# Renewing sixteen operands eight slots apart instead of six, in a kernel of attention and Fourier mixing

## The chip, the core and the metric

The kernel runs on one core of a Trainium2 chip. The metric is the device time of one execution in microseconds (us): three runs before the change took 1754.96, 1755.81 and 1759.93, median 1755.81. One further execution was profiled: it took 1751.4, of which 1749.6 lie between its first and last instruction (the span) and 1.8 around them. All engine times below are of this one execution.

Engines are named as in the profile: PE multiplies matrices, DVE, ACT and POOL work on elements (VectorE, ScalarE, GpSimd), SP issues transfers. Each takes its own instructions in the order in which the program holds them.

## What is computed

Two mixings of the same `x` (2048 rows of 512, float32), joined by a gate per row:

```python
q, k, v = split(x @ wqkv)                          # 32 heads of 16
o = softmax(q @ k.T * scale) @ v                   # over all 2048 keys
a = o @ wo
re, im = x @ dft_hid_re.T, x @ dft_hid_im.T        # spectral part
b = dft_seq_re @ re - dft_seq_im @ im
g = sigmoid((x * gate_w).sum(-1))
out = g * a + (1 - g) * b
```

## The kernel before

**Stages.** The first 292 us or so project q, k and v and the hidden transforms `re` and `im`, which are stored in memory as `ab_d[0]` and `ab_d[1]` (sixteen row blocks of 128 rows each). Then the spectral products run until about 693 us of the span, and the attention over all heads follows until the end. Both earlier stages also carry scans: the maximum of every row of scores is needed before the softmax, and the products and maxima for it are placed beside the other work.

**Operands in two parts.** Every float32 operand is split in a rounded part and the rest of it (`ah`, `al`, or `hi`, `lo`), and a product is the sum of three: hi*hi, hi*lo, lo*hi. ACT copies the rounded part, DVE or POOL subtracts it from the raw operand.

**The spectral loop** (L551) goes over units of coefficients. A unit is 512 columns of one row block `t` of the cosine matrix (phase 0) or the sine matrix (phase 1), and is multiplied with four operands `s` (L585 to L589), three products each; so a unit is twelve products. POOL splits the coefficients three units ahead (L552, L313, L314), SP fetches them eight ahead (L553, L305). After the last unit of a row block ACT scales the two halves of the sum (tx and ty, L598, L602), and POOL adds them and, in phase 1, the stored sum of phase 0 (L546, L548).

**The change of parts.** The sixteen operands of phase 0 (`re`) lie in blocks which those of phase 1 (`im`) take over. So that blocks come free early, the last two row blocks of phase 0 and the first two of phase 1 are done by halves: (14, 0), (14, 1), (15, 0), (15, 1), then (14, 2), (14, 3), (15, 2), (15, 3), then in phase 1 (0, 0), (0, 1), (1, 0), (1, 1), and (0, 2), (0, 3), (1, 2), (1, 3), each pair being row block and quarter of the operands. In row block 15 (`swap`, L575) operand `s` has had its last use of phase 0, and its renewal is put on a list.

**Slots.** `beside()` is called once after each product (L589) and counts a slot. It first runs what is due (`run_due`, L208, by due slot and then by order of entry), then places the scan work. `after(n, f)` (L203) makes `f` due n slots later. What is due is only *placed* in its engine's order at that point; it then runs when that engine reaches it. Below, slot 0 is the start of unit (15, 0), whose first product is slot 1; phase 1 begins after slot 72.

**A renewal** (`renew`, L577) places three things: the copy `ah[s]` on ACT (L580), four slots later the subtraction `al[s]` on DVE (on POOL for s = 3, 7, 11, 15; L581, shown at L215 by the profile), and for s = 8 to 12 the load of operand s + 3 on SP (L286). Operands 0 to 7 are loaded ahead into two tiles (`early`, L570 to L574), 8 to 10 at slot 24 (L592, L593). Loads of 8 to 15 share three buffers (`abr`), so the load of s + 3 waits for the subtraction of s, and what stands behind that load in SP's order waits too.

**The scans beside.** About every third slot a scan is placed (`scan_folded`, L136): two score products on PE (L149), ACT's rectified copy of one into `fold` (L153), and DVE's addition and running maximum with the next (L155). Four score banks, `d0`, `d1`, `k0`, `k1`, have one buffer each: a product for a `d` bank waits for ACT's copy of two scans before, one for a `k` bank for DVE's maximum of two scans before. When a head pair's scans are complete, four small instructions finish its maxima on DVE (`shift`, L158: L170 to L173), four slots apart; one such group falls into this stretch, at slots 21, 25, 29 and 33.

Of the kernel before, what the change touches and what calls it, by code (L numbers as in the profile page):

```python
# [46 lines left out]
def build(tc, x, xT, wqkv, wo, wrT, wiT, cr, ci, gate, out):  # L47
    nc = tc.nc
    with ExitStack() as ctx:
# [34 lines left out]
        def row_loads(p, queue, keys=k_d):  # L84

            qs = stk.tile([P, S], F32R, tag="stk", name="qs")
            ks = stk.tile([P, S], F32R, tag="stk", name="ks")
            loads = []
            for j in range(2):
                b, r = 64 * j, slice(DH * ((2 * p + j) % 8), DH * ((2 * p + j) % 8) + DH)  # L90
                loads += [(ks[b:b + 32, :], keys[p // 4][r, 0:1, :].to_broadcast([DH, 2, S])),
                          (qs[b:b + 32, :], q_d[p // 4][r, :, :].rearrange("e n s -> (e n) s")),
                          (ks[b + 32:b + 48, :], keys[p // 4][r, 1, :]),
                          (qs[b + 32:b + 48, :], q_d[p // 4][r, 0, :])]
            return (qs, ks), [lambda dst=dst, src=src: queue.dma_start(dst.bitcast(F32), src) for dst, src in loads]
# [7 lines left out]
        def load_use(p):  # L103
            if p < NP:
                used[p], loads = row_loads(p, nc.sync)
                for load in loads:
                    load()
                qs, ks = used[p]
                for j in range(2):
                    b = 64 * j + 48  # L110
                    nc.sync.dma_start(ks[b:b + 2, :].bitcast(F32), ones_d)
                    for n in range(2):
                        nc.sync.dma_start(qs[b + n:b + n + 1, :].bitcast(F32),
                                          m_d[p][n:n + 1, :, j].rearrange("n g b k -> n b g k"))
# [61 lines left out]
        def halves_of(ps, lhs, rhs, first, last):  # L176

            for j in range(2):
                r = slice(64 * j, 64 * j + 64)
                nc.tensor.matmul(ps[j], lhs[r], rhs[r], start=first, stop=last)  # L180

        def block(i):
            return big.tile([P, 512], F32R, tag=f"b{i}", name=f"b{i}")
# [6 lines left out]
        with ExitStack() as pf:  # L190
# [8 lines left out]
            def xy():  # L199
                ps = psf.tile([P, 2, 512], F32, tag="xy", name="xy")  # L200
                return ps[:, 0, :], ps[:, 1, :]

            def after(n, f, *args):  # L203

                count[0] += 1
                due.append((slots[0] + n, count[0], f, args))
# [15 lines left out]
            def scan_at(spacing):  # L222
                pace[0] = spacing

            def beside():

                slots[0] += 1
                run_due()
                if pace[0] is None:
                    return  # L230
                pace[1] += (PACE / FOLD_PACE if seen[0] in FOLDED else 1.0) / pace[0]
                if seen[0] == FOLDED[0] and not beds:
                    pace[1] = 0.0
                while seen[0] < FRONT and pace[1] >= 1.0:
                    pace[1] -= 1.0
                    n = seen[0]
                    if n % SCANS == 36 and n - n % SCANS + SCANS < FRONT:
                        load_scan_beside(n // SCANS + 1)
                    if n not in FOLDED:
                        done = scan_plain(n)  # L240
                    else:

                        scan_folded(n, 0, *beds)
                        done = behind(n - 1)
                    seen[0] += 1
                    if seen[0] == FRONT:
                        done = behind(n)
                    if done is not None and done % SCANS == SCANS - 1:
                        for d, part in enumerate(shift(done // SCANS)):
                            after(3 + 4 * d, part)  # L250
# [33 lines left out]
            def load_operand(ph, s, pool):  # L284
                raw = pool.tile([P, D], F32, tag="raw", name="abr", bufs=3)
                nc.sync.dma_start(raw, ab_d[ph][s])  # L286
                return raw
# [19 lines left out]
            def prepare(n, copy=nc.gpsimd.tensor_copy, sub=nc.gpsimd.tensor_sub):  # L307
                if n >= len(coef):
                    return
                hi, lo = (cw.tile([P, 512], F32R, tag=tag, name=tag + "_").rearrange("p (c q) -> p c q", q=P)  # L310
                          for tag in ("chi", "clo"))
                raw = craw.pop(n)
                copy(hi, raw)  # L313
                sub(lo, raw, hi.bitcast(F32))  # L314
                ready[n] = hi, lo
# [212 lines left out]
            with ExitStack() as py:  # L528
                cp = py.enter_context(tc.tile_pool(name="cp", bufs=2, reuse_waits="tile"))
                def fetch(n):  # L530
                    if n < len(coef):
                        load_coef(n, cp.tile([P, CS, P], F32, tag="craw", name="craw", bufs=5))
# [18 lines left out]
                for n, (ph, t, u) in enumerate(coef):  # L551
                    prepare(n + 3)  # L552
                    fetch(n + 8)  # L553
                    if u == 0 and (ph, t) == (0, NB - 1):
                        scan_at(NARROW)
                    if u == 2 and (ph, t) == (1, 0):
                        scan_at(PACE)
                    if n == len(coef) - 2 * NU:
                        unfolded[FRONT // SCANS], loads = row_loads(FRONT // SCANS, nc.sync)
                        for load in loads:  # L560
                            load()
                        load_use(0)
                    hi, lo = ready.pop(n)
                    if u == 0:
                        pss[t] = xy()
                        if ph:
                            yre[t] = cp.tile([P, D], F32, tag="yre", name="yre")
                            nc.sync.dma_start(yre[t], y_d[t // 4][:, t % 4, :])
                    if (ph, t, u) == (0, NB - 3, 0):
                        for i in range(2):  # L570
                            raw = stk.tile([P, 4, D], F32, tag="stk", name="early")
                            for d in range(4):
                                early[4 * i + d] = raw[:, d, :]
                                nc.sync.dma_start(raw[:, d, :], ab_d[1][4 * i + d])  # L574
                    swap = (ph, t) == (0, NB - 1)  # L575

                    def renew(s):  # L577
                        raw = early.pop(s)
                        ah[s], al[s] = block(2 * s), block(2 * s + 1)
                        nc.scalar.copy(ah[s], raw)  # L580
                        after(4, (nc.gpsimd if s % 4 == 3 else nc.vector).tensor_sub, al[s], raw, ah[s].bitcast(F32))  # L581
                        if s >= 8 and s + 3 < NB:
                            early[s + 3] = load_operand(1, s + 3, cp)

                    for w in range(CS):  # L585
                        s = u * CS + w
                        for i, (c_, a_) in enumerate(((hi, ah[s]), (hi, al[s]), (lo, ah[s]))):
                            halves_of(pss[t], c_[:, w, :], a_, s == 0 and i == 0, s == NB - 1 and i == 2)
                            beside()  # L589
                        if swap:  # L590
                            if s == 7:
                                for i in range(8, 11):  # L592
                                    early[i] = load_operand(1, i, cp)  # L593
                            after(1 + 3 * (s % 8), renew, s)
                    if u == NU - 1:
                        tx = cp.tile([P, D], F32, tag="tx", name="tx")
                        ty = cp.tile([P, D], F32, tag="ty", name="ty")
                        nc.scalar.mul(tx, pss[t][0], gm[:, t:t + 1])  # L598
                        if n == len(coef) - 1:
                            nc.vector.tensor_scalar_mul(ty, pss[t][1], gm[:, t:t + 1])  # L600
                        else:
                            after(5, nc.scalar.mul, ty, pss[t][1], gm[:, t:t + 1])  # L602
                        after(10, mixed, ph, t, yre.get(t), tx, ty)
# [405 lines left out]
```

## Time and profile before

| | us |
|---|---|
| median of three runs | 1755.81 |
| profiled execution, its time | 1751.4 |
| its span | 1749.6 |
| PE busy in the span | 1719.9 |
| ACT busy | 1451.9 |
| DVE busy | 1155.1 |
| POOL busy | 712.7 |

The profile's timeline lists, per engine, start, duration, line and operation, what is written from what, how many alike were merged, and in square brackets the idle time ahead with what ended it. The table by windows gives, for a stretch of the span, each engine's busy time and instructions, and the TensorE clock that was granted (1.00 is full speed). Two score products or two half products run side by side on PE, so a row with x2 is one pair.

### The profile page before, as it was taken

What the parts mean: (1) busy time and instruction counts of PE and PEld (TensorE: products, weight loads), DVE (VectorE), ACT (ScalarE), POOL (GpSimd) and SP (SyncE); (2) the same over time, 40 slices, a digit from 0 to 9 for tenths busy, and PEclk for the clock granted to TensorE, in tenths of its full rate; (3) what the DMA queues carried; (4) which work ended last, traced back from release to release, by engine and by line L of the source; (5) the groups of instructions that cost most, each with busy time, mean ns of one, the idle gap of its engine ahead of it and who ended that gap; (6) DMA issues with size and microseconds to landing.
All of it is one profiled execution on the core that took longest, in us unless ns stands there. A gap on an engine that the chain in (4) does not pass through costs nothing.

```text
span 1749.6 us, 35589 instructions
## 1 busy us (share of the span) xinstructions
PE 1719.9 (98%) x13640; PEld 1021.8 (58%) x13640; DVE 1155.1 (66%) x1876; ACT 1451.9 (83%) x2384; POOL 712.7 (41%) x814
## 2 busy tenths in 40 slices
PE   8999999999999999999999999999999999999998
PEld 6887787888888887333333333333334555555554
DVE  6799999999999887666666666666664212222333
ACT  5445346888887887999999999999999888888885
POOL 3678667555556664032322323232232322322222
PEclk9999999999999999999999999999999999999999
DMA  8782666434354445433232423515313254255612
GB/s 296 254 298 79 190 201 206 121 115 117 104 154 140 139 133 120 74 59 63 58 67 56 82 40 64 95 23 99 78 35 73 64 118 90 68 141 137 177 36 100
DMA packets 126810, 199.55 MB, mean 114 GB/s; under 512 B 54016, under 2 KB 56560, under 8 KB 119728
## 3 DMA queue, kind: packets, MB, share of 16 engines
q1 hardware_dynamic: 84368, 161.02, 34.4%
q0 software_dynamic: 38496, 19.47, 5.2%
q10 hardware_dynamic: 3776, 16.78, 3.6%
q8 instruction: 107, 1.75, 0.4%
q14 instruction: 63, 0.52, 0.1%
HBM read 133.04 MB, written 63.71 MB: 112 GB/s over the span
## 4 chain that ended last, share of the span: by engine, by line
PE 89%; DMA 3%; DVE 3%; POOL 2%; issue 2%; ACT 1%; SPq 0%; DVEq 0%; ACTq 0%; POOLq 0%
PE pvb L660 28%; PE xy L180 21%; PE s L645 19%; PE s L180 8%; PE s L149 7%; PE s L130 6%; DVE mx L132 1%; DMA fa<-ks_d 1%; DMA kf_d<-fa 1%; POOL s L215 1%; DMA raws<-wqkv 0%; DMA raws<-xT 0%; POOL el L215 0%; POOL fa L215 0%; DMA abr<-ab_d 0%
## 5 line engine op out<-in xcount | busy, mean ns | idle before, releaser
L132 DVE TENSOR_REDUCE mx<-s 128x2 f32<-128x1024 f32 x524 | 627.2, 1222 | 207.5 <-PE s L130 207.4
L649 ACT ACTIVATE eb<-s 128x1024 f32<-128x1024 f32 x512 | 579.3, 1131 | 55.1 <-PE s L645 55.1
L653 ACT ACTIVATE e<-s 128x512 f32<-128x512 f32 x1024 | 610.3, 708 | 0.4 <-PE s L645 0.4
L660 PE MATMUL pvb<-e,va 128*17 128x512 f32 x2048 | 517.3, 598 | 0.0
L660 PE MATMUL pvb<-eb,va 128*17 128x512 f32 x2048 | 517.1, 598 | 0.0
L645 PE MATMUL s<-qs,ks 50*128 50x512 f32 x2048 | 428.1, 438 | 2.3 <-DVE ty L600 1.6
L645 PEld LDWEIGHTS s<-qs,ks 50*128 50x128 f32 x2048 | 212.6, 185 | 372.4 <-ACT eb L649 282.6
L155 DVE CUSTOM_DVE_ANT_0 fold<-s,fold 128x512 f32<-128x512 f32 x500 | 339.1, 690 | 39.0 <-PE s L149 19.4
L153 ACT ACTIVATE fold<-s 128x512 f32<-128x512 f32 x500 | 296.1, 602 | 70.0 <-PE s L149 43.1
L149 PE MATMUL s<-ks,qs 48*128 48x512 f32 x1000 | 223.3, 404 | 7.6 <-DVE mx L155 6.1
L130 PE MATMUL s<-ks,qs 48*128 48x512 f32 x1048 | 221.6, 396 | 3.7 <-DVE mx L132 2.5
L668 POOL DMA_DIRECT2D lc<-ob x124 | 63.1, 515 | 308.2 <-DVE ob L665 307.9
L660 PEld LDWEIGHTS pvb<-eb,va 128*17 128x17 f32 x2048 | 69.2, 96 | 190.2 <-issue 182.0
L149 PEld LDWEIGHTS s<-ks,qs 48*128 48x128 f32 x1000 | 120.9, 184 | 47.6 <-DVE mx L155 18.2
L675 POOL DMA_DIRECT2D r_d<-lc x31 | 18.1, 585 | 294.9 <-DVE lc L674 286.0
L130 PEld LDWEIGHTS s<-ks,qs 48*128 48x128 f32 x1048 | 108.3, 184 | 14.9 <-DVE mx L132 6.0
L180 PE MATMUL xy<-w,b 64*128 64x512 f32 x768 | 105.2, 392 | 0.2 <-ACT s L379 0.2
L401 ACT ACTIVATE tx<-xy 128x512 f32<-128x512 f32 x48 | 28.7, 599 | 78.6 <-PE xy L180 52.5
L754 DVE SCALAR_TENSOR_TENSOR y<-s,g,y 128x512 f32<-128x512 f32 x50 | 36.6, 748 | 76.6 <-PE s L180 76.0
L677 POOL DMA_DIRECT2D rb<-r_d x124 | 60.6, 496 | 63.0 <-DMA r_d<-lc 63.0
L180 PE MATMUL s<-b,chi 64*128 64x512 f32 x542 | 85.2, 390 | 0.3 <-ACT chi L963 0.3
L180 PEld LDWEIGHTS xy<-w,b 64*128 64x128 f32 x768 | 72.5, 186 | 17.6 <-ACT s L379 1.0
(750 smaller groups left out, 2320.4 us busy)
## 6 DMA issues: line engine op xcount, KB each, us to landing
craw<-ci SPq DMA_DIRECT2D x64, 256.0 KB
craw<-cr SPq DMA_DIRECT2D x60, 256.0 KB
ks<-k_d SPq DMA_DIRECT2D x46, 256.0 KB
qs<-q_d SPq DMA_DIRECT2D x46, 256.0 KB
ab_d<-ab SPq DMA_DIRECT2D x32, 256.0 KB
y_d<-y SPq DMA_DIRECT2D x32, 256.0 KB
o_d<-oh POOLq DMA_DIRECT2D x28, 256.0 KB, 9.8
o_d<-ol POOLq DMA_DIRECT2D x28, 256.0 KB, 11.9
```

The costliest lines, as they stand in the source:

```text
L130: nc.tensor.matmul(ps[:, j, :], qs[b:b + 48, qb * P:(qb + 1) * P], ks[b:b + 48, c * 512:(c + 1) * 512], start=True, stop=True)
L132: nc.vector.tensor_reduce(mx[p][:, :, qb, c], ps, axis=AX.X, op=ALU.max)
L149: nc.tensor.matmul(ps, qs[b:b + 48, qb * P:(qb + 1) * P], ks[b:b + 48, c * 512:(c + 1) * 512], start=True, stop=True)
L153: nc.scalar.activation(fold[j], ps, AF.Relu)
L155: nc.vector.tensor_tensor_reduce(out=fold[j], in0=ps, in1=fold[j], scale=1.0, scalar=-3.0e38, op0=ALU.add, op1=ALU.max, accum_out=mx[p][:, ...
L180: nc.tensor.matmul(ps[j], lhs[r], rhs[r], start=first, stop=last)
L645: nc.tensor.matmul(pss[j], ks[b:b + 50, kb * P:(kb + 1) * P], qs[b:b + 50, q0:q0 + 512], start=True, stop=True)
L649: nc.scalar.activation(e, ps, AF.Exp, scale=SCALE)
L653: nc.scalar.activation(e[j], pss[j], AF.Exp, scale=SCALE)
L660: nc.tensor.matmul(pvb[r:r + VC, :], va[:, kb, 2 * p + j, :], es[c][j], start=kb == 0, stop=kb == NB - 1, tile_position=(0, r))
L668: nc.gpsimd.dma_start(lc[32 * n:32 * n + 32, :], ob[r + DH:r + VC, :].rearrange("p (s e) -> p s e", e=16))
L677: nc.gpsimd.dma_start(rb[r:r + DH, :], r_d[p][h][n:n + 1, :].to_broadcast([DH, 512]))
```

## The change

The due slot of a renewal goes from `1 + 3 * (s % 8)` to `1 + 5 * (s % 8)` slots after the operand's last use. The last uses are themselves three slots apart, so successive renewals of a group of eight lie eight slots apart instead of six.

```diff
                         if swap:
                             if s == 7:
                                 for i in range(8, 11):
                                     early[i] = load_operand(1, i, cp)
-                            after(1 + 3 * (s % 8), renew, s)
+                            after(1 + 5 * (s % 8), renew, s)
```

The copies fall due at these slots; each subtraction follows four slots behind its copy:

| s | 0 | 1 | 2 | 3 | 4 | 5 | 6 | 7 | 8 | 9 | 10 | 11 | 12 | 13 | 14 | 15 |
|---|---|---|---|---|---|---|---|---|---|---|---|---|---|---|---|---|
| before | 4 | 10 | 16 | 22 | 28 | 34 | 40 | 46 | 52 | 58 | 64 | 70 | 76 | 82 | 88 | 94 |
| after | 4 | 12 | 20 | 28 | 36 | 44 | 52 | 60 | 52 | 60 | 68 | 76 | 84 | 92 | 100 | 108 |

The number of instructions on each engine and the order of PE's products do not change. On SP the load of operand 14 comes to stand behind the store of a finished row block, a load of coefficients and the load of a stored sum, where it stood ahead of the three.

## The prediction

> **What bounds the kernel now.** I read the busy shares, then the chain that ended last, then the table by windows around the change of parts.
>
> ```profile
> span 1749.6 us, 35589 instructions
> ...
> PE 1719.9 (98%) x13640; PEld 1021.8 (58%) x13640; DVE 1155.1 (66%) x1876; ACT 1451.9 (83%) x2384; POOL 712.7 (41%) x814
> ...
> PE 89%; DMA 3%; DVE 3%; POOL 2%; issue 2%; ACT 1%; SPq 0%; DVEq 0%; ACTq 0%; POOLq 0%
> ```
>
> ```profile
> 534.00:576.00 42.00, 38.69 (x306) 32.01 (x303) 36.41 (x93) 31.39 (x58) 27.26 (x25) 0.96 0.43 136
> 576.00:618.00 42.00, 42.00 (x359) 36.82 (x356) 37.86 (x116) 35.30 (x62) 26.72 (x26) 1.00 0.45 128
> 618.00:660.00 42.00, 40.94 (x344) 34.18 (x341) 36.86 (x112) 33.57 (x58) 24.28 (x25) 1.00 0.48 133
> ```
>
> PE sets the time nearly everywhere. The columns are length, then PE, weight loads, DVE, ACT, POOL, clock, transfers. The renewals lie in the first window. There PE does 306 matmuls against 359 in the next window of the same length; it idles 3.3 us, and the granted clock is 0.96. So in this stretch others pace PE, and what is lost here is about the most that the change can win. Behind it PE is close to full, so a PE that is early at 576 should stay early.
>
> The loss shows in the scan pairs on PE, one per three slots:
>
> ```profile
> 533.71 0.48 PE L149 MATMUL s<-ks,qs 48*128 48x512 f32 x2
> ...
> 534.65 0.48 PE L149 MATMUL s<-ks,qs 48*128 48x512 f32 x2
> ...
> 538.41 0.48 PE L149 MATMUL s<-ks,qs 48*128 48x512 f32 x2
> ...
> 539.81 0.68 PE L149 MATMUL s<-ks,qs 48*128 48x512 f32 x2 [0.23 <-DVE mx L155]
> ...
> 544.67 0.78 PE L149 MATMUL s<-ks,qs 48*128 48x512 f32 x2
> ...
> 547.75 0.51 PE L149 MATMUL s<-ks,qs 48*128 48x512 f32 x2 [1.59 <-DVE mx L155]
> ...
> 568.62 0.40 PE L149 MATMUL s<-ks,qs 48*128 48x512 f32 x2
> ...
> 571.21 0.50 PE L149 MATMUL s<-ks,qs 48*128 48x512 f32 x2 [1.49 <-ACT fold L153]
> ```
>
> ```profile
> 545.50:549.00 3.50, 1.91 (x15) 1.30 (x13) 3.50 (x8) 1.06 (x3) 1.54 (x1) 1.00 0.22 68
> 549.00:552.50 3.50, 3.50 (x20) 3.07 (x18) 2.44 (x7) 2.04 (x5) 0.72 (x2) 0.53 0.08 18
> ```
>
> Undisturbed, pairs start 0.94 apart. The pair at 533.71 is slot 3, the one at 571.21 slot 102: 33 steps, 31.0 us undisturbed and 37.5 here. So 6.5 us are lost: 0.46 ahead of 539.81 (a step of 1.40), 2.14 ahead of 547.75 (3.08), 1.65 ahead of 571.21 (2.59), about 1.6 to a clock of 0.53 through 3.5 us right behind the second gap (3.5 x 0.47), and some 0.7 in steps that are 0.1 too long.
>
> **The change part by part.** No instruction is added or removed; sixteen copies, sixteen subtractions and five loads shift by up to 14 slots, 4.4 us at 0.94 per three. Operand 7 now falls due for subtraction at slot 64 and is needed from slot 94 on, operand 15 at slot 112 and from 142 on: 30 slots, 9.4 us, cover the lateness itself, so it costs nothing. If that cover were gone, each slot of lateness would cost PE 0.31. What counts is who stands beside whom.
>
> *The gaps at 539.8 and 547.7* come from DVE:
>
> ```profile
> 537.78 1.37 DVE L215 TENSOR_TENSOR b<-early,b 128x512 fp32r<-128x512 f32 x1
> ...
> 543.02 1.27 DVE L172 CAST chi<-mt 128x32 fp32r<-128x32 f32 x1
> ...
> 544.82 1.09 DVE L215 TENSOR_TENSOR b<-early,b 128x512 fp32r<-128x512 f32 x1
> 545.84 1.25 DVE L173 TENSOR_TENSOR clo<-mt,chi 128x32 fp32r<-128x32 f32 x1
> 547.01 0.68 DVE L155 CUSTOM_DVE_ANT_0 fold<-s,fold 128x512 f32<-128x512 f32 x1
> ```
>
> ```profile
> 537.30 1.30 POOL L314 TENSOR_TENSOR clo__8425<-craw,chi__8424 128x512 fp32r<-128x512 f32 x1
> ...
> 542.96 1.30 POOL L215 TENSOR_TENSOR b<-early,b 128x512 fp32r<-128x512 f32 x1
> 544.76 0.61 POOL L313 CAST chi__8571<-craw 128x512 fp32r<-128x512 f32 x1 [0.50 <-PE xy L180]
> 545.45 1.59 POOL L314 TENSOR_TENSOR clo__8572<-craw,chi__8571 128x512 fp32r<-128x512 f32 x1
> ```
>
> ```profile
> L215 DVE TENSOR_TENSOR b<-early,b x6: 679/685/1374, 535.9 to 550.1; 128x512 fp32r<-128x512 f32 x6
> ```
>
> The last row is least, median and most in ns. A subtraction that takes 0.68 alone takes 1.09 and 1.37 where POOL is at work, and two tiny instructions of 32 columns take 1.25 and 1.27. Each ends at or just behind POOL's: 537.30 + 1.30 = 538.60, and DVE's ends 0.55 later at 539.15; 542.96 + 1.30 = 544.26, DVE's at 544.29; 545.45 + 1.59 = 547.04, DVE's at 547.09. So the two engines exclude each other on such instructions, and whoever starts second waits. (The Trainium skill says so too: GPSIMD Engine Reference, section 1, Specifications, has POOL share its SBUF interfaces with DVE, with contention for DVE instructions of two SBUF inputs or in a two-port mode. By this rule alone the wider spacing is no cure, since only POOL's place beside DVE decides; that speaks against the change, and the new meetings below carry it.)
>
> With eight slots, operand 1 is subtracted at slot 16 instead of 14, behind one more maximum, and by then POOL's 537.30 is over: the 0.46 goes. Operand 4 leaves slot 32 for 40. L173 then takes the place of 544.82, waits for POOL's 0.61 at most and is done by about 545.5, and the maximum of 547.01 starts 1.5 earlier. Against that, operand 2 moves from slot 20, where POOL idled, to 24, where POOL starts on coefficients (a unit's end): 0.4 to 1.3 more, by the rows 1.09 - 0.68 and 1.30. Walking DVE's order on from there, L172 still meets POOL's subtraction of operand 3, the maxima run late, and PE loses 0.2 at slot 30 and 0.7 at slot 36. So 2.14 becomes 0.9; bounds 0 and 2.14.
>
> *The slow clock* followed the 1.59 us gap; no gap of the walk is over 1.2. It goes: 1.6, bounds 0 and 1.6. (The Trainium skill, TensorE: Matmul & The Clock Gate, Part 1, has the clock halve after an idle window of about 3.4 us on a free-running grid. Here a gap half as long was followed by it, and the one of 1.49 at 569.7 was not, so the measurement decides on the length; the grid may be what tells the two apart, and is a rival below.)
>
> *The gap at 571.2* is a load that came too late, for operand 15 on ACT:
>
> ```profile
> 561.88 1.31 POOL b L215
> ...
> 565.26 4.75 DMA abr<-ab_d
> ```
>
> ```profile
> 570.04 0.62 ACT L580 CAST b<-abr 128x512 fp32r<-128x512 f32 x1 [2.22 <-DMA abr<-ab_d]
> ```
>
> The chain names it: POOL's subtraction of operand 11 frees a buffer, SP may go on at 563.2, issues a store and two loads, and only then the load that took 4.75. ACT waits 2.22, folds queue behind it, and PE waits for a bank. Now the load of s + 3 and its copy lie 24 slots apart instead of 18, 1.9 us more, and the load of 15 follows that of 14 directly instead of three issues later, with its buffer free at slot 88 and its copy at slot 108. That is 6.2 us less about 0.7 for the subtraction, against 4.75: the 1.65 goes. Bounds 0 and 1.65.
>
> *What is new:* at slots 52 and 60 two copies stand together (6 with 8, 7 with 9), at 56 two subtractions on DVE, since the second group of eight starts before the first has ended.
>
> ```profile
> L580 ACT CAST b<-abr 128x512 fp32r<-128x512 f32 x8 | 5.0, 629 | 2.5 <-DMA abr<-ab_d 2.5
> ...
> L546 POOL TENSOR_TENSOR y<-tx,ty 128x512 f32<-128x512 f32 x2 | 3.3, 1666 | 0.5 <-ACT ty L215 0.4
> ```
>
> ACT's second copy adds 0.63 ahead of a fold for which PE has about 0.2 of slack: 0.45. On DVE the second subtraction adds 0.68, and near it lie POOL's L546 of 1.67 and a coefficient split: one more meeting, then the maximum two scans later is 0.7 late at slot 72; 0.2 besides for the second double copy. I take 1.4; bounds 0.3 (the cover holds but for ACT) and 3.2 (both pairs meet L546 or a split in full, 2 x 1.3, plus 0.6).
>
> The sum: 0.46 + (2.14 - 0.9) + 1.6 + 1.65 - 1.4 = 3.5 us less. The profiled execution would take 1751.4 - 3.5 = 1747.9. The runs' median lies 4.4 above it, for reasons no row shows; I take the same difference from it: 1755.8 - 3.5 = 1752.3.
>
> **The rivals.** *All of the loss goes.* If DVE at slots 24 and 56 starts just ahead of POOL instead of behind it (the walk has them within 0.1 us of each other), neither new queue reaches PE: 1755.8 - 6.5 = 1749.3. For it: the slower median may hold a slow clock behind the third gap too, which would be won as well. Against it: POOL was busy 27.3 of the 42 us, so few places are free.
>
> *The load is late anyway.* SP holds the loads of 14 and 15 in order, and 14 waits for POOL's subtraction of 11, which could itself slip behind a coefficient split and L546. Then 1.65 stays: 1754.0. Against it: 1.9 us more of lead, and three issues fewer ahead of the load of 15, cover the 2.22 that it lacked.
>
> *The clock falls by its grid,* wherever PE has gaps of about a microsecond: 1.6 stays, 1753.9. For it: not every long gap was followed by a slow clock.
>
> *Slower.* The double renewals at slots 52 to 60 stall PE as the crowding at 547.7 did. It decides once a gap there reaches about 1.6: two such, each with its slow clock, cost 2 x (2.14 + 1.6) = 7.5; with the 0.9 before them 8.4 against the 6.5 lost now, so 1757.7. For it: tx, ty and L546 of row block 14 fall in the same slots. Against it: eight slots instead of six between the other renewals leave DVE more room to catch up.
>
> **How the numbers follow.** Forecast 0.42, all goes 0.30, load late 0.08, clock 0.08, slower 0.12. About 0.3%, 5.3 us, is what a measurement of this kernel can tell from no change: below 1750.5 is faster, above 1761.1 slower. Faster: most of "all goes" (0.26) and a fifth of the forecast, by the low bounds of its new costs (0.09), 0.35. Slower: half of the last case, where a third gap follows, 0.06. The rest, 0.59, is no change. The range from 1748 to 1757.7 ends at the two outer cases, with a little for the runs' scatter at the low end.
>
> **What would show it.** After the change, the step ahead of L173 should be near 1 us instead of 3.08, no window in the stretch should have a clock under 0.9, no copy on ACT should wait for a load, and the pairs from slot 3 to 102 should take 34 us instead of 37.5. Small gaps should stand at slots 30 to 36 and 57 to 72. A copy at L580 that still waits, a clock of 0.53, or a gap over 1.5 behind slot 52 would each take its term out. A gain here that is gone at the attention's start would make the step from PE to the end wrong.

## The result and the profile after

The changed kernel took 1748.56 us in the median of twelve runs (1746.07 to 1751.81), the kernel before 1756.53 (twelve runs, 1749.63 to 1759.93). The two medians lie 8.0 apart. The ratio, which is not that of the medians, is 0.9963, with a 95% interval of 0.9953 to 0.9973: 6.5 us less, 4.7 to 8.3 by the interval. The profiled execution took 1747.04; its span is 1745.2.

From the page of the changed kernel, the span and the shares of the chain that ended last:

```profile
span 1745.2 us, 35588 instructions
...
PE 87%; DVE 5%; DMA 2%; issue 2%; POOL 2%; ACT 1%; SPq 0%; DVEq 0%; ACTq 0%; POOLq 0%
```

The table by windows, for the two windows that were shown of before (length, PE, weight loads, DVE, ACT, POOL, clock, transfers):

```profile
534.00:576.00 42.00, 40.66 (x335) 35.29 (x334) 39.03 (x101) 33.95 (x63) 29.66 (x28) 1.00 0.48 151
576.00:618.00 42.00, 42.00 (x358) 37.61 (x356) 37.64 (x116) 35.10 (x62) 27.26 (x27) 1.00 0.46 130
```

PE now does 335 matmuls in the window of the renewals instead of 306, its idle time falls from 3.3 to 1.3 us, and the clock is full. The scan pairs on PE, from the timeline of the changed kernel, with slot 3 at 534.84 and slot 105 at 569.67:

```profile
534.84 0.50 PE L149 MATMUL s<-ks,qs 48*128 48x512 f32 x2
...
539.52 0.52 PE L149 MATMUL s<-ks,qs 48*128 48x512 f32 x2
540.46 0.52 PE L149 MATMUL s<-ks,qs 48*128 48x512 f32 x2
...
545.14 0.55 PE L149 MATMUL s<-ks,qs 48*128 48x512 f32 x2
546.09 0.54 PE L149 MATMUL s<-ks,qs 48*128 48x512 f32 x2
...
551.84 0.45 PE L149 MATMUL s<-ks,qs 48*128 48x512 f32 x2
553.28 0.50 PE L149 MATMUL s<-ks,qs 48*128 48x512 f32 x2 [0.29 <-ACT fold L153]
...
567.83 0.40 PE L149 MATMUL s<-ks,qs 48*128 48x512 f32 x1
568.87 0.50 PE L149 MATMUL s<-ks,qs 48*128 48x512 f32 x1 [0.65 <-DVE mx L155]
569.67 0.40 PE L149 MATMUL s<-ks,qs 48*128 48x512 f32 x1
```

The step ahead of slot 21 (539.52 to 540.46) is 0.94 and the one ahead of slot 39 (545.14 to 546.09) 0.95: the first two gaps are gone, and the third with its late load. New are 0.5 ahead of slot 60 (553.28), 0.3 and 0.4 ahead of slots 75 and 81, and 0.5 and 0.9 ahead of slots 99 and 105 (567.83 to 569.67; x1 is half a pair, and the first half counts). From slot 3 to slot 105 it is 34.8 us; the pair of slot 105 before the change started at 572.25, which makes 38.5. The stretch is 3.7 us shorter.

The late load shows on SP and ACT. SP issues the loads of operands 14 and 15 (the last row, x2) behind the load of coefficients and that of a stored sum, and the copies of both run without a wait for a load:

```profile
560.47 1.48 SPq L305 DMA_DIRECT2D craw<-ci  x1
562.00 0.42 SPq L568 DMA_DIRECT2D yre<-y_d  x1
562.53 3.29 SPq L286 DMA_DIRECT2D abr<-ab_d  x2
```

```profile
568.06 0.61 ACT L580 CAST b<-abr 128x512 fp32r<-128x512 f32 x1
...
570.85 0.61 ACT L580 CAST b<-abr 128x512 fp32r<-128x512 f32 x1
```

Between the two profiled executions the rest adds up like this. The changed kernel reaches slot 3 1.1 us later (533.71 and 534.84); the clock was slow in it between 26 and 32 and between 190 and 196 us, in code that is the same in both, and whether that is all of the 1.1 is not shown. From slot 105 to the first score product of the attention it is 122.8 before and 122.7 after, so nothing of the gain is lost there. Then the clock is slow before the change and not after it, at the attention's start:

```profile
690.00:700.00 10.00, 7.67 (x49) 4.14 (x46) 3.69 (x4) 4.71 (x7) 3.02 (x3) 0.80 0.12 39
700.00:710.00 10.00, 10.00 (x70) 3.58 (x70) 5.13 (x5) 8.08 (x13) 0.00 (x0) 0.86 0.83 146
```

```profile
690.00:700.00 10.00, 7.56 (x55) 2.97 (x51) 5.72 (x6) 7.51 (x12) 3.02 (x3) 1.00 0.44 103
700.00:710.00 10.00, 10.00 (x76) 3.67 (x74) 6.54 (x6) 10.00 (x17) 0.00 (x0) 1.00 0.52 82
```

The first pair of rows is of before, the second of after; from there to the end it makes 1.8. In sum 1.1 - 3.7 - 1.8 = -4.4, the difference of the spans. Whether the 1.8 belongs to the change, and why the runs gained 6.5 and the profiles 3.7 where the change lies, was for the experiments.

### The profile page after: what moved, and what is told of

The parts are those of the page before. It is cut to its first block, busy times and chain, and to the rows that moved or that the text cites. A ratio compares the mean times of both kernels' runs of the same rounds, so it can differ in the third digit from the quotient of the medians.

```text
span 1745.2 us, 35588 instructions
## 1 busy us (share of the span) xinstructions
PE 1718.2 (98%) x13640; PEld 1031.1 (59%) x13640; DVE 1152.3 (66%) x1876; ACT 1451.5 (83%) x2384; POOL 711.2 (41%) x814
## 4 chain that ended last, share of the span: by engine, by line
PE 87%; DVE 5%; DMA 2%; issue 2%; POOL 2%; ACT 1%; SPq 0%; DVEq 0%; ACTq 0%; POOLq 0%
PE pvb L660 28%; PE xy L180 21%; PE s L645 18%; PE s L180 8%; PE s L149 7%; PE s L130 6%; DVE mx L132 3%; DMA lc<-ob 1%; POOL s L215 1%; POOL el L215 0%; DVE fold L155 0%; DMA q_d<-el 0%; DMA fa<-ks_d 0%; DMA raws<-wqkv 0%; DVE s L215 0%
## 5 line engine op out<-in xcount | busy, mean ns | idle before, releaser
L149 PE MATMUL s<-ks,qs 48*128 48x512 f32 x1000 | 233.1, 404 | 5.6 <-DVE mx L155 5.1
L130 PE MATMUL s<-ks,qs 48*128 48x512 f32 x1048 | 221.2, 396 | 5.1 <-DVE mx L132 3.1
L149 PEld LDWEIGHTS s<-ks,qs 48*128 48x128 f32 x1000 | 126.8, 184 | 42.7 <-DVE mx L155 16.2
L130 PEld LDWEIGHTS s<-ks,qs 48*128 48x128 f32 x1048 | 108.4, 184 | 17.1 <-DVE mx L132 8.1
```

The source lines that it names most:

```text
L130: nc.tensor.matmul(ps[:, j, :], qs[b:b + 48, qb * P:(qb + 1) * P], ks[b:b + 48, c * 512:(c + 1) * 512], start=True, stop=True)
L149: nc.tensor.matmul(ps, qs[b:b + 48, qb * P:(qb + 1) * P], ks[b:b + 48, c * 512:(c + 1) * 512], start=True, stop=True)
```

## The experiments

The theory: three gaps of one stretch, each with a cause of its own, were removed, and their sum less some new costs is the gain. The rivals differ by experiment. "Stretch" is the time from the pair of slot 3 to that of slot 105 in the run's profile, against 38.5 in the first profile of before and 34.8 in that of after; losses are what a step takes over 0.94.

**The kernel before, again.** No edit.

> The unchanged kernel, for a second profile and for the scatter. Theory: the three gaps of the first profile are the program's own, so the pairs from slot 3 to slot 105 take 38.5 us again plus or minus 2, with gaps ahead of the pairs of slots 39 and 102; how often the clock goes slow behind them differs from run to run, and since the runs' median lies 4.4 us over the profiled run, a slow clock stands behind the gap of slot 102 too in some runs (then 40). Rival: the gaps are an accident of one execution, and the stretch takes 36 or less here. Ratio 1.000 either way.

Ratio 1.0005 (0.9994 to 1.0017). The stretch took 40.6, its third gap was much longer, and the clock was slow behind it too. From this run's timeline (PE, then ACT), its chain and its table by windows:

```profile
547.22 0.50 PE L149 MATMUL s<-ks,qs 48*128 48x512 f32 x2 [1.58 <-DVE mx L155]
...
571.88 0.79 PE L149 MATMUL s<-ks,qs 48*128 48x512 f32 x2 [2.67 <-ACT fold L153]
```

```profile
570.71 0.62 ACT L580 CAST b<-abr 128x512 fp32r<-128x512 f32 x1 [3.40 <-DMA abr<-ab_d]
```

```profile
564.82 5.87 DMA abr<-ab_d
```

```profile
570.50:576.00 5.50, 4.12 (x22) 3.34 (x24) 2.18 (x7) 3.02 (x6) 1.89 (x3) 0.69 0.38 124
```

The load of operand 15 took 5.87 here, where it had taken 4.75. So ACT waited 3.40 instead of 2.22, PE lost 2.83 instead of 1.65 ahead of slot 102, and through 570.5 to 576 the clock was 0.69 on average. Up to slot 111, with the slow steps behind, the way is 43.1 us; it was 40.4 in the first profile, and it is 36.7 in the changed kernel. By this profile the change is worth 6.4, by the first one 3.7. That is a likely reason why the runs gained more than the first pair of profiles: the execution that the prediction was built on had the shorter load. How often the longer one comes, two profiles cannot tell.

**Only the first eight operands eight slots apart.**

```diff
-                            after(1 + 3 * (s % 8), renew, s)
+                            after(1 + (5 if s < 8 else 3) * (s % 8), renew, s)
```

> Only operands 0 to 7 lie eight slots apart, 8 to 15 six. Theory: the gap of slot 39 and its slow clock go (0.46 + 2.14 + 1.6), the load of operand 15 stays late (1.65 stays), the double copies at slots 52 and 58 to 60 cost 0.5 to 1: the stretch from slot 3 to 105 takes 38.5 - 4.2 + 0.8 = 35 us, ratio 0.998. Rival, that the gain came from the loads: the stretch stays at 38 and the ratio at 1.000.

Ratio 0.9971 (0.9961 to 0.9981). The stretch took 35.7. The losses of slots 21 and 39 are gone with the slow clock, and 1.38 stay ahead of slot 102, with two copies that wait 0.54 and 1.95 for loads. The doubles cost 0.50 at slot 60, and 0.99 followed at slot 75, together more than the 0.5 to 1 expected.

```profile
568.46 0.50 PE L149 MATMUL s<-ks,qs 48*128 48x512 f32 x2 [1.22 <-ACT fold L153]
```

**Only the last eight eight slots apart.**

```diff
-                            after(1 + 3 * (s % 8), renew, s)
+                            after(1 + (3 if s < 8 else 5) * (s % 8), renew, s)
```

> Only operands 8 to 15 lie eight slots apart, 0 to 7 six. Theory: the gap of slot 39 stays, with a slow clock behind it in most runs, no copy waits for a load any more (1.65 goes), and the late subtractions of operands 12 and 13 cost about 1 again as in the changed kernel: the stretch takes 38 us, ratio 0.9995. Rival, that the gain came from the loads and a slow clock behind that gap: 35 us or so and ratio 0.997.

Ratio 0.9979 (0.9968 to 0.9989). The stretch took 37.7: no copy waits for a load, 2.17 stay ahead of slot 39, with a slow clock behind them (1.6 over three steps).

```profile
547.60 0.50 PE L149 MATMUL s<-ks,qs 48*128 48x512 f32 x2 [1.60 <-DVE mx L155]
```

The stretch is as long as the theory had it, but in part by luck. Operands 12 and 13 cost nothing here: the steps ahead of slots 99 and 105 take 0.94 and 0.93. Instead 1.2 were lost ahead of slots 75 and 81, where the subtractions of operands 9 and 10 take 1.51 and 1.55 beside POOL's split. The ratio is lower than 0.9995. That fits the run of the kernel before: against a load as late as there, with a slow clock behind it, the load's cure is worth more than the 1.65 that I had for it. Each half alone is a clear gain, and the profiles show that each removes losses which the other leaves.

**One subtraction moved, spacing of six.**

```diff
-                        after(4, (nc.gpsimd if s % 4 == 3 else nc.vector).tensor_sub, ...)
+                        after(12 if s == 4 else 4, (nc.gpsimd if s % 4 == 3 else nc.vector).tensor_sub, ...)
```

> Spacing of six, but the subtraction of operand 4 alone falls due eight slots later, at slot 40 instead of 32. Theory, that one meeting of DVE and POOL made the gap: L173 ends before POOL's split begins, the step ahead of slot 39 falls from 3.1 us to about 1.2 and no slow clock follows: the stretch takes 38.5 - 3.6 = 35 us, ratio 0.998. Rival, that DVE simply had too much to do at six slots: the gap only moves to slots 42 to 51, the stretch stays at 38, ratio 1.000.

Ratio 0.9982 (0.9971 to 0.9993). DVE's timeline of this kernel shows the meeting go:

```profile
545.68 1.28 DVE L172 CAST chi<-mt 128x32 fp32r<-128x32 f32 x1
...
547.49 0.60 DVE L173 TENSOR_TENSOR clo<-mt,chi 128x32 fp32r<-128x32 f32 x1
548.02 0.68 DVE L155 CUSTOM_DVE_ANT_0 fold<-s,fold 128x512 f32<-128x512 f32 x1
...
551.71 1.12 DVE L215 TENSOR_TENSOR b<-early,b 128x512 fp32r<-128x512 f32 x1
```

L173 takes 0.60 instead of 1.25, PE loses 0.49 instead of 2.14 ahead of slot 39, and no slow clock follows. A part of the rival holds as well: the subtraction of operand 6 meets POOL at 551.71, and 0.88 are lost ahead of slot 51. The stretch as a whole took 39.0 and not 35, because the load of operand 15 took 6.45 in this profile and cost 3.43 ahead of slot 102, with a slow clock behind it:

```profile
573.43 0.79 PE L149 MATMUL s<-ks,qs 48*128 48x512 f32 x2 [3.28 <-ACT fold L153]
```

So one meeting made most of the gap ahead of slot 39; about half of the 1.65 that was won there came back twelve slots later.

**The changed kernel, again.** No edit.

> The changed kernel again, for a second profile and for the scatter. Theory: stretch from slot 3 to 105 in 35 us plus or minus 1, no slow clock in it, no copy that waits for a load; whether a slow clock follows the turn to the attention differs from profile to profile, so it is back in this one or not, without meaning for the change. Ratio to the kernel before 0.996 to 0.997. Rival, that the change also cures the slow clock at the attention's start: that is absent again.

Ratio 0.9979 (0.9966 to 0.9992). The stretch took 34.8 again, with the same losses to within 0.04 us, no slow clock and no wait for a load. At the attention's start the clock was slow this time:

```profile
690.00:700.00 10.00, 7.68 (x45) 3.92 (x43) 3.69 (x4) 4.71 (x7) 3.01 (x3) 0.79 0.18 58
700.00:710.00 10.00, 10.00 (x70) 3.61 (x70) 5.43 (x5) 8.42 (x13) 0.00 (x0) 0.87 0.79 127
```

In ten of the eleven profiles of this case, over all kernels, the clock goes slow at this place; the first profile of the changed kernel is the exception. So the 1.8 us of the first comparison of profiles is no steady part of what the change does.

**Four buffers for the loads, spacing of six.**

```diff
-                raw = pool.tile([P, D], F32, tag="raw", name="abr", bufs=3)
+                raw = pool.tile([P, D], F32, tag="raw", name="abr", bufs=4 if ph else 3)
```

> Spacing of six, but the loads of operands 8 to 15 share four buffers instead of three, so a load no longer waits for the subtraction just before it. Theory: the gap of slot 39 and its slow clock stay as they are, the gap of slot 102 and any slow clock behind it go: stretch from slot 3 to 105 in 37 us, ratio 0.998. Rival, that the last load is late because the transfers themselves are slow at that time: the copy of operand 15 still waits 1 us or more, ratio 0.9995.

Ratio 0.9986 (0.9973 to 0.9999), stretch 37.5. Between theory and rival: the loss ahead of slot 102 falls to 0.61 without a slow clock, but the copy of operand 15 still waits 1.00, and those of 13 and 14 wait 0.38 and 0.28.

```profile
563.13 5.83 DMA abr<-ab_d
```

The load starts earlier, at 563.13 instead of 565.26 of the first profile, and takes 5.83 instead of 4.75, so it lands only 1.1 earlier. Both when SP issues it and how long it then takes make it late.

**All sixteen copies eight slots apart, none beside another.**

```diff
-                            after(1 + 3 * (s % 8), renew, s)
+                            after(1 + 5 * (s % 8) + (16 if s > 7 else 0), renew, s)
```

> Spacing of eight, and the second eight operands sixteen slots later still, so that all sixteen copies lie eight slots apart from slot 4 to slot 124 and none stands beside another. Theory, that the double copies of the changed kernel cost 0.5 us and its late subtractions beside POOL the rest: 0.5 less at slot 60, but meetings of DVE and POOL elsewhere, since eight slots against POOL's twelve per unit meet at some renewals whatever the start: stretch in 34 us plus or minus 1, ratio to the kernel before 0.996. Rival, that the doubles cause the late losses as well: stretch in 33, ratio 0.995.

Ratio 0.9976 (0.9963 to 0.9989); the median, 1747.4, and that of the changed kernel on the same chip, 1748.4, are not told apart. The stretch took 32.5, near the 32.0 of 34 steps of 0.94, with one loss over 0.1 (0.35 at slot 99). That is past my theory, and past the rival too; but the renewals of this kernel run on to slot 128, behind the stretch. Two subtractions still meet POOL. From the timelines of DVE, POOL (the split beside the second) and PE:

```profile
562.50 1.47 DVE L215 TENSOR_TENSOR b<-abr,b 128x512 fp32r<-128x512 f32 x1
...
573.17 1.60 DVE L215 TENSOR_TENSOR b<-abr,b 128x512 fp32r<-128x512 f32 x1
```

```profile
572.93 1.29 POOL L314 TENSOR_TENSOR clo__9047<-craw,chi__9046 128x512 fp32r<-128x512 f32 x1
```

```profile
573.46 0.59 PE L149 MATMUL s<-ks,qs 48*128 48x512 f32 x2
...
575.43 0.50 PE L149 MATMUL s<-ks,qs 48*128 48x512 f32 x2 [0.92 <-DVE mx L155]
```

The second falls behind the stretch, where pairs may follow at 0.70: the step to 575.43 takes 1.97, so 1.27 are lost. From slot 105 to the first score product of the attention it is 123.9 here and 122.7 in the changed kernel. Of the 2.3 us by which the stretch is shorter than the changed kernel's, half comes back there; from slot 3 to the attention it is 156.4, against 157.6 in the changed kernel and 161.3 before. A meeting delays DVE by 0.8 to 0.9; how much PE loses by it, 0.35 or 1.27 here, depends on what else DVE has just then.

**Seven slots apart.**

```diff
-                            after(1 + 3 * (s % 8), renew, s)
+                            after(1 + 4 * (s % 8), renew, s)
```

> Spacing of seven. Theory, that single meetings and the load's lead decide and not the spacing as such: the load of operand 15 has 21 slots less 0.7 us of lead, 5.9 us for 4.8 of transfer, so no copy waits; whether L173 meets operand 4's subtraction at slot 36 is past it by three, so the gap of slot 39 is under 1: stretch in 35 to 36 us, ratio 0.997. Rival, that the gain grows with the room between renewals: halfway, 36.7 us, ratio 0.998, with a wait for the last load left.

Ratio 0.9982 (0.9970 to 0.9995). A miss for the theory: the stretch took 37.5, and a copy still waits, as the rival had it.

```profile
567.61 0.62 ACT L580 CAST b<-abr 128x512 fp32r<-128x512 f32 x1 [1.85 <-DMA abr<-ab_d]
```

```profile
561.65 5.94 DMA abr<-ab_d
```

The gap of slot 39 is 0.61, as expected. The late copy and its load are those of operand 14, not of 15. ACT was ready for it at 565.76, 4.1 behind the issue at 561.65, so the lead was 4.1 and not 5.9, and a load of 4.75 would have been late too. This is what the prediction's rival of the late load had named: the buffer came free only when POOL had subtracted operand 11, at 561.23, behind a split of coefficients, and SP had the load of a stored sum to issue just then. With eight slots between the last operands no copy waited in any of five profiles; in the two of the changed kernel the copy of operand 14 ran 5.5 and 6.0 behind the issue of its load.

**The changed kernel with two subtractions later.**

```diff
-                        after(4, (nc.gpsimd if s % 4 == 3 else nc.vector).tensor_sub, ...)
+                        after(8 if s in (12, 13) else 4, (nc.gpsimd if s % 4 == 3 else nc.vector).tensor_sub, ...)
```

> The changed kernel, with the subtractions of operands 12 and 13 alone four slots later (slots 92 and 100 instead of 88 and 96). Theory: in the changed kernel both meet POOL's split of coefficients (1.62 and 1.63 us instead of 0.69), and this makes its losses of 0.5 ahead of slot 99 and 0.9 ahead of slot 105; four slots later POOL is past its split, both subtractions take 0.7 to 1.1, and the two losses fall from 1.4 to 0.3 together: slot 3 to 105 in 33.7 us instead of 34.8, ratio to the kernel before 0.997. Rival, that DVE is too full there at any place: the losses move to slots 105 to 111 and the way from slot 3 to 111 stays at 36.7.

Ratio 0.9963 (0.9950 to 0.9975), stretch 33.4. DVE's timeline, first of the changed kernel, then of this one:

```profile
563.82 1.62 DVE L215 TENSOR_TENSOR b<-abr,b 128x512 fp32r<-128x512 f32 x1
...
566.58 1.63 DVE L215 TENSOR_TENSOR b<-abr,b 128x512 fp32r<-128x512 f32 x1
```

```profile
563.67 0.69 DVE L215 TENSOR_TENSOR b<-abr,b 128x512 fp32r<-128x512 f32 x1
...
566.29 0.69 DVE L215 TENSOR_TENSOR b<-abr,b 128x512 fp32r<-128x512 f32 x1
```

Both take 0.69, the losses ahead of slots 99 and 105 are gone, and none came in their place: from slot 3 to 111 it is 35.3 instead of 36.7. The theory holds here; the late losses of the changed kernel are two meetings with POOL's split. From slot 3 to the attention it is 156.2, no more than the 156.4 with all copies apart.

## Why the prediction was right

The median, 1748.56, lies in the range given, near its low end; the forecast of 1752.3 was 3.7 too high. The gain forecast, 3.5, is about half of the 6.5 measured and lies under its interval; the range held because its low end had been set by the rival by which all goes (1749.3), so for the size of the median it was luck. The change is faster by 0.37% (0.27 to 0.47 by the interval), just past the bound of 0.3%, which had been given a chance of 0.35. For the profiled execution the forecast was 1747.9, and it took 1747.04; of the 4.4 that it gained, 3.7 lie in the stretch, where 3.5 stood.

**The gap ahead of slot 21.** Right: 0.46 became nothing.

**The gap ahead of slot 39.** Right in its cause for the most part, as the experiment with operand 4 alone shows. The 0.9 set against it did not come: in the walk L172 met POOL, while in the trace it took 0.17 and L173 0.83, and no step from slot 21 to 39 lost 0.1.

**The slow clock.** Right: no window of the stretch in the changed kernel is slow, in two profiles.

**The late load.** Right in that it went: no copy waits in either profile of the changed kernel. Its size is the term that was furthest off. I took 1.65 from one execution, in which the transfer took 4.75. Other profiles with six slots between the last operands had 4.63, 5.83, 5.87 and 6.45 for it, and the two longest waits of PE, 2.67 and 3.28, had a slow clock behind them: there the loss was 2.83 and 3.43, and 1.5 to 1.6 more in slow steps. Of the four profiles with this lead and three buffers two show a small loss (1.38 and 1.65) and two a large one. Which is the usual one is not shown; the gain of 6.5 in the first comparison speaks for the large one, and so does the last eight alone, which gained 3.7 by its ratio with 1.2 of new losses against it; the second comparison, also 3.7 by its ratio, does not. The rival by which all goes had named this ("the slower median may hold a slow clock behind the third gap too"), and it is what the repeated profile shows.

The longer lead was not all of the cure either. The sum counted that a store and two loads no longer stand ahead of the load of operand 15; it set no price on their standing ahead of that of 14. The kept traces hold when each load landed. In the two profiles of the kernel before, the load of 15 took 4.75 and 5.87 and that of 14 took 2.89 and 2.56; in the two of the changed kernel, that of 15 took 3.15 and 2.48 and that of 14 took 5.07 and 4.23. So the long transfer passed on to operand 14, whose copy came 5.5 and 6.0 behind the issue: in the first of the two it was in time by half a microsecond. Why a load behind that store and the two loads takes longer is not shown.

**The new costs.** I took 1.4 for the doubles. At slot 60 ACT's double copy cost 0.5 (0.45 foreseen), at slots 75 and 81 0.7 were lost where 0.7 stood for slot 72. Not foreseen were 1.4 at slots 99 and 105, from operands 12 and 13 beside POOL's split: the walk had not been carried past slot 78. Together 2.6, against 2.3 in the sum (0.9 and 1.4): the sum came out at 3.5 for 3.7 in part because two errors of its own cancelled, which is luck. From slot 3 to 102 it took 33.0, where 34 stood.

**The rivals.** That all goes came nearest in time, but not by its way: 2.6 of new losses stand in the stretch. The load late anyway, and the clock by its grid, fell: neither was seen in the changed kernel, though the first is what happened at seven slots. The slower case fell too; its doubles cost 0.5 to 1.2, not a gap of 1.6.

**Behind the stretch.** Right: 122.8 and 122.7 us from slot 105 to the attention.

What stays open is the exact size in the runs: the two comparisons of the same kernels gave 0.9963 and 0.9979, whose intervals overlap, and slow clocks elsewhere in the program move single runs by more than the difference.

## What to carry to other kernels

Take the price of a late transfer from several profiles: one profiled execution showed a loss of 1.65 us where a second of the same kernel showed 2.83 and a slow clock, and runs that are slower than the profiled one can be a sign of it. When work is spread out in an engine's order, check where each piece then falls beside the other engine that excludes it, through the whole stretch, since a spacing cures one meeting and makes another. And measure past the place where the moved work ends: with the second group started when the first was done, the stretch looked 2.3 us better, and half of that came back behind it.

## What the runs showed of the hardware

Pauses of PE of little more than 1.5 us were followed by a clock of about half for some 3.5 us. In this stretch, over the profiles of all kernels, six waits of 1.58, 1.59, 1.60, 1.60, 2.67 and 3.28 us were followed by a slow clock, and three of 1.09, 1.22 and 1.49 were not. (The Trainium skill, TensorE: Matmul & The Clock Gate, Part 1, states an idle window of about 3.4 us; here pauses of half that length were followed by it.) It is no sharp bound: at the attention's start PE waited 1.62 or 1.63 in every profile, and a slow clock followed in ten of the eleven, but not in the first of the changed kernel.

The load of operand 15, 256 KB, took 4.75 and 5.87 us in two executions of the same kernel, and from 4.63 to 6.45 over all five profiles with six slots between the last operands.
